# A spectral block on one Trainium2 core: the inverse DFT on 32x64 tiles, the second forward DFT on 64x64 tiles

## The chip, the cores and the metric

The kernel runs on one core of a Trainium2 chip. The metric is device time in microseconds, the median of several executions. Engine names below: TensorE (PE; its weight loads are PEld), VectorE (DVE), ScalarE (ACT), GpSimd (POOL), SyncE (SP, which here only issues DMAs).

## The reference, cut

```python
# x: 4096 rows of 640, all float32
mod = (silu(c) @ w_mod).reshape(1, 6, 1, 640)        # sa, ca, ga, sb, cb, gb
h = layernorm(x) * (1 + ca) + sa
Z = rfft(h, axis=rows).reshape(2049, 4, 160)         # 4 blocks of 160 columns
hr = relu(Z.real @ w1[0] - Z.imag @ w1[1] + b1[0])   # per block, 160 x 160
hi = relu(Z.imag @ w1[0] + Z.real @ w1[1] + b1[1])
or_ = softshrink(hr @ w2[0] - hi @ w2[1] + b2[0], 0.01)
oi_ = softshrink(hi @ w2[0] + hr @ w2[1] + b2[1], 0.01)
x = x + ga * irfft(or_ + 1j * oi_, n=4096)
h = layernorm(x) * (1 + cb) + sb
x = x + gb * ((silu(h @ w_gate) * (h @ w_up)) @ w_down)   # 640 -> 1728 -> 640
```

## The kernel before

The 4096 rows are written as 128 x 32, so that each DFT over rows is done in two factors with a twiddle matrix in the second. The first forward factor (128 points) follows the layer norm and its results go to DRAM (`s1`). Then comes a loop over 8 chunks of frequencies and 4 blocks of columns; a step p is one pair, `ch = p // 4` and `b = p % 4`. The order of instructions on each engine in this part is written out by hand in the loop. The pieces of a step, with the names that the profile shows:

- `load_g` (L310, tile g, SyncE) brings one chunk's rows from `s1`. Partitions hold 32 values of n2 times (parity, real or imaginary part).
- `stage_b(ch, t)` (L636, tile pb), for t = 0 to 4 (four blocks of 128 columns, and the four remainders of 32 columns as t = 4), is the second forward factor: 4 fp32 matmuls of 128 rows, 128 stationary columns and 128 moving columns. An fp32 matmul shows as two records. Its weights are the data; the moving operand is the twiddle table `tb`, which is zero where parities differ. The PSUM bank is b0, or b1 for t = 4.
- `evac_b` (L643 on ScalarE, L644 on VectorE, tile z) scales and splits the result into a high part in fp32r and a remainder. `rem_high`, `rem_low` (L686, L690, tile rt) do it for t = 4, whose rows then go through DRAM to other partitions (`rem_move`, `rem_read`); in the first two chunks `evac_rh`, `evac_rl` (L666, L676, tile rz) do it in place.
- `stage_l1` (L732, tile pl) is the first product: 21 fp32r matmuls into two banks of tag p1 and one of p3. ScalarE takes h (L749, L750) and u (L763) from them, VectorE the low parts (L751) and u (L764); `tail_l1` makes r2.
- `stage_l2` (L800, tile pc, tag p2) is the second product of the step before: 16 fp32r matmuls of 320 columns, two PSUM tiles, each added to the bias into tile tt on VectorE (L802).
- `move_x` (L821, tile xx, SyncE) moves tt by eight DMAs for each chunk, so that real and imaginary parts of 64 frequencies lie on the 128 partitions of one of four tiles xx.
- `shrink_parts` (L827, L828, ScalarE) and `shrink` (L833, or L835 and L836, VectorE) are the soft threshold of one xx; `shrink_high` (L842, ScalarE) and `shrink_low` (L847, VectorE) split it into xh and xl.
- `stage_i` (L858 to L860, tile pi, tag p3) is the first inverse factor of one xx: two halves of 320 columns, each 3 fp32r matmuls with the table `bm` (high and low part). ScalarE evicts to co (L861), and POOL issues the write to DRAM, `s2` (L862).

In a step p of the loop TensorE runs `stage_l1(p)`, `stage_b` of the next chunk (one call, two where b = 1), small sums for the modulation, `stage_l2(p - 1)` and `stage_i(p - 7)`. ScalarE, VectorE and SyncE follow the written order as well; each engine does its queue in order.

The last chunk differs: its inverse runs in fp32 from tt without a move (`inverse_last`, L906, on 64-row halves), in two halves of columns; the first rows of the output are made at once (`first_y`, tile py, L1089 to L1094) with a folded table that takes the last chunk's frequencies straight from tt and the others from `s2` through `load_first_rows` (tile cf, L913, SyncE). `first_stats` and `first_norm` (L1118) normalise them for the FFN, whose first transposes are L1926.

The FFN stage after it is ordered by a planner in the program with costs and due times of its own. It is the larger part of the time.

PSUM has eight banks: two buffers each of p1, p2, p3, and b0 and b1.

Of the kernel before, what the change touches and what calls it, by code (L numbers as in the profile page):

```python
# [6 lines left out]
F32 = mybir.dt.float32  # L7
# [39 lines left out]
def constants():  # L47
# [38 lines left out]
    tb = tb.transpose(0, 3, 1, 2, 4, 5, 6).reshape(8, 4, 128, 128)[ORDER].reshape(32, 128, 128)  # L86
# [3 lines left out]
    tx = tx.transpose(2, 0, 1, 3).reshape(128, 2)  # L90
# [20 lines left out]
    bm = bm.reshape(2, 128, 128)  # L111
    bi = bm[1].reshape(2, 64, 128)

    bx = np.tile(bm[1].reshape(2, 64, 128).transpose(1, 0, 2), (2, 1, 1)).reshape(128, 256)
    bmh, bml = _hl(bm)
    bm = np.stack([bmh, bml], axis=1)
    bm = np.ascontiguousarray(bm.transpose(2, 0, 1, 3)).reshape(128, 2 * 2 * 128)
# [12 lines left out]
    for n in range(4):  # L130
        for h in range(2):
            for r in range(2):
                for i in range(2):
                    m = 4 * (4 * ORDER[-1] + 2 * h + i)
                    ge[64 * i:64 * i + 64, n, 256 * h + 128 * r:256 * h + 128 * r + 128] = (
                        bi[r].reshape(64, 4, 32)[:, :, n] @ ga[n, m:m + 4])
        ge[:, n, 512:] = ga[n]
# [9 lines left out]
        "k_bm": f(bm),  # L147
# [24 lines left out]
def body(tc, x, w1, b1, w2, b2, wg, wu, wd, c, wm, k_fa, k_tb, k_tx, k_bm, k_bx, k_ga, k_ge, k_id, out, dbg=None):  # L172
# [29 lines left out]
    with ExitStack() as top:  # L202
# [3 lines left out]

        def bank0(i, shape, name):
            return ps.tile(shape, F32, tag=f"b{i % 2}", bufs=1, name=name)
# [28 lines left out]
        with ExitStack() as af:  # L237
# [4 lines left out]
            bm = wp.tile([P, 2, 2, 128], F32R, name="bm")  # L242
# [53 lines left out]
            def load_tb(ch):  # L296
                tb = lp.tile([P, 4, 128], F32, tag="tb", bufs=2, name=f"tb{ch}")
                nc.sync.dma_start(tb, k_tb[:, 4 * ch:4 * ch + 4])
                tbs[ch] = tb


            def load_g(ch, lo=0, hi=32, dma=None, cols=(slice(0, D),)):
# [6 lines left out]
                for e in cols:  # L309
                    (dma or nc.sync).dma_start(gs[ch][4 * lo:4 * hi, :, e], src[:, lo:hi, :, e].rearrange("q n j d -> n q j d"))  # L310
# [22 lines left out]
            with tc.tile_pool(name="sp", bufs=1) as sp:  # L333
# [176 lines left out]

            hp = af.enter_context(tc.tile_pool(name="hp", bufs=1, reuse_waits="tile"))
# [20 lines left out]
            bx = p2.tile([P, 2, 128], F32, name="bx")  # L532
# [9 lines left out]
            nc.sync.dma_start(bx.rearrange("p a b -> p (a b)"), k_bx)  # L542
# [17 lines left out]
            def mod_sum(m, hf=0):  # L560
# [3 lines left out]
                elif m in (2, 5):  # L564
                    if m == 5:
                        gbb.append(low_p.tile([P, 320], F32, tag="m", bufs=4, name=f"gbb{hf}"))
                    pm = (bank0(1, [P, 512], f"pm{m}_{hf}") if hf else
                          ps.tile([P, 512], F32, tag="p3", name=f"pm{m}_{hf}"))
                    mm(pm[:, :320], ones, acc[:, 320 * hf:320 * hf + 320], start=True, stop=True)
                    act.activation(gab[:, 320 * hf:320 * hf + 320] if m == 2 else gbb[hf], pm[:, :320], AF.Copy)  # L570
                else:
                    pm = bank0(m, [P, 512], f"pm{m}")
# [55 lines left out]

            def stage_b(ch, t):
                g, tb = gs[ch], tbs[ch]  # L630
                tag = {(0, 1): "p2", (1, 1): "p3"}.get((ch, t))
                pb = (ps.tile([P, 2, 256], F32, tag=tag, name=f"pb{ch}_{t}") if tag else
                      bank0(1 if t == 4 else 0, [P, 2, 256], f"pb{ch}_{t}"))
                col = slice(128 * t, 128 * t + 128)
                for j in range(4):
                    mm(pb[:, :, 64 * j:64 * j + 64], g[:, j, col], tb[:, j, :], start=True, stop=True)  # L636
                pbs[ch, t] = pb

            def evac_b(ch, t):
                pb = pbs[ch, t]  # L640
                z = lp.tile([P, 2, 2, 258], F32R, tag="z", bufs=4, name=f"z{ch}_{t}")
# [4 lines left out]
                if ch == CE:  # L646
                    pool.tensor_copy(z[:, 0, :, 0:257:256], f32(edge[:, 0, t]))
# [10 lines left out]
            def evac_rh(ch, b):  # L658
                pb = pbs[ch, 4]
# [5 lines left out]
                for i in range(2):  # L665
                    act.activation(rzs[ch][32 * i:32 * i + 32, b, 0:256], pb[q, i, :], AF.Identity,  # L666
                                   scale=ca1[q, 4:5])

            def evac_rl(ch, b):
                pb = pbs[ch, 4]  # L670
                r = rzs[ch]
                q = slice(32 * b, 32 * b + 32)
                for i in range(2):
                    rh = slice(32 * i, 32 * i + 32)
                    rl = slice(64 + 32 * i, 96 + 32 * i)
                    dve.scalar_tensor_tensor(r[rl, b, 0:256], pb[q, i, :], ca1[q, 4:5],  # L676
                                             f32(r[rh, b, 0:256]), op0=OP.mult, op1=OP.subtract)
# [6 lines left out]
            def rem_high(ch):  # L684
                rt = rts[ch] = low_p.tile([P, 2, 2, 258], F32R, tag="wt", name=f"rt{ch}")
                act.activation(rt[:, 0, :, 0:256], pbs[ch, 4], AF.Identity, scale=ca1[:, 4:5])  # L686

            def rem_low(ch):
                rt = rts[ch]
                dve.scalar_tensor_tensor(rt[:, 1, :, 0:256], pbs[ch, 4], ca1[:, 4:5], f32(rt[:, 0, :, 0:256]),  # L690
                                         op0=OP.mult, op1=OP.subtract)
# [16 lines left out]
            def stage_l1(ch, b, later=None):  # L708
                NN = width(ch)
                z = zs[ch, b]  # L710
# [4 lines left out]
                for o in range(2):  # L715
# [3 lines left out]
                    seqs.append([(w1a[:, b, cs], z[:, 0, 0, :NN]), (w1a[:, b, cs], z[:, 1, 0, :NN]),  # L719
                                 (w1a[:, b, cl], z[:, 0, 0, :NN]),  # L720
# [241 lines left out]
            for p in range(LAST + 1):  # L962
# [3 lines left out]
                if p < 4:  # L966
                    for f, *a in mods.get(p, ()):
                        f(*a)
# [1596 lines left out]
```

## Time and profile before

| | us |
|---|---|
| median of 3 runs | 1437.01 |
| lowest, highest | 1436.25, 1438.35 |
| span of the profiled execution | 1434.9 |
| spectral stage up to the first forward call of `stage_b` | 0 to 52 |
| loop and tail of the spectral stage | 52 to 311 |
| FFN | 311 to 1435 |

Of the profiled execution only its span is given; launch and end lie around it. In the views, a row has the start or the busy time, the line of the kernel, the operation with the names of its tiles (out<-in), partitions x elements, and a count. In brackets stands how long the engine was idle before it and what ended that. "issue" is time in which the engine waited for nothing that the profile shows. PE records overlap, since their ends are modelled: the distance between starts is what a record costs.

### The profile page before, as it was taken

How to read it: one execution, taken by the hardware profiler on the slowest of the kernel's cores; microseconds unless marked ns; L12 is line 12 of the kernel's file. 1: busy time of each engine (PE TensorE's matmuls, PEld its weight loads, DVE VectorE, ACT ScalarE, POOL GpSimd, SP SyncE). 2: the span in 40 equal slices, each digit the busy share in tenths (PEclk: the TensorE clock that was granted, in tenths of full speed). 3: DMA queues.
4: the chain of work that ended last, by engine and by line, in shares of the span. 5: the costliest groups of instructions: out<-in, count | busy, mean ns of one | idle time of the engine just before them, and what ended most of it. 6: DMA issues, size and time to landing. Idle time of an engine off the chain costs nothing.

```text
span 1434.9 us, 23925 instructions
## 1 busy us (share of the span) xinstructions
PE 1401.5 (98%) x8516; PEld 1327.5 (93%) x8516; DVE 1097.0 (76%) x1978; ACT 783.8 (55%) x1560; POOL 538.0 (37%) x641
## 2 busy tenths in 40 slices
PE   6899999989999999999999999999999999999999
PEld 2699999968989889899999999999999999999998
DVE  8878888778887687767888778888647768567775
ACT  7868878735545555545555556554435345245432
POOL 5300311154444444323244434434324555146533
PEclk9999999999999999999999999999999999999999
DMA  9988798658677989897887997778796666966652
GB/s 377 322 271 259 242 290 275 218 172 263 232 244 277 339 278 298 323 353 243 279 287 253 343 369 251 253 264 290 280 334 233 208 217 240 359 216 222 207 186 89
DMA packets 187383, 382.28 MB, mean 266 GB/s; under 512 B 22240, under 2 KB 104736, under 8 KB 185472
## 3 DMA queue, kind: packets, MB, share of 16 engines
q1 hardware_dynamic: 179072, 364.37, 74.4%
q0 software_dynamic: 6608, 13.77, 3.0%
q10 hardware_dynamic: 1584, 2.62, 0.5%
q8 instruction: 67, 1.10, 0.3%
q14 instruction: 52, 0.43, 0.1%
HBM read 266.66 MB, written 104.86 MB: 259 GB/s over the span
## 4 chain that ended last, share of the span: by engine, by line
PE 78%; DVE 10%; DMA 7%; ACT 2%; issue 1%; SPq 1%; POOL 1%; DVEq 0%; ACTq 0%; POOLq 0%
PE pd L2435 14%; PE pw L2116 8%; PE pw L2118 8%; PE pw L2117 8%; PE pd_X L2297 5%; PE pc L800 4%; PE pl L732 3%; PE pg L1981 3%; PE pg L1980 3%; PE pg L1982 3%; PE pd_Y L2297 3%; PE pw L2127 2%; PE pw L2129 2%; PE pw L2128 2%; DVE st_a L193 2%; DVE wb L1457 2%
## 5 line engine op out<-in xcount | busy, mean ns | idle before, releaser
L2435 PE MATMUL pd<-wdh,a 128*128 128x320 f32 x1040 | 239.2, 310 | 0.6 <-DVE x L2407 0.6
L2435 PEld LDWEIGHTS pd<-wdh,a 128*128 128x128 f32 x1040 | 176.3, 188 | 1.2 <-DVE x L2407 0.9
L2435 PE MATMUL pd<-wdl,a 128*128 128x320 f32 x540 | 166.2, 309 | 0.0
L1457 DVE TENSOR_TENSOR wb<-r,wb 128x512 fp32r<-128x512 f32 (+3 forms) x154 | 155.9, 1023 | 12.0 <-ACT wb L1454 10.3
L2116 PE MATMUL pw<-h,wt 128*128 128x384 f32 x416 | 141.2, 340 | 2.2 <-ACT s_x L2135 2.2
L2118 PE MATMUL pw<-h,wt 128*128 128x384 f32 x416 | 140.2, 337 | 0.0
L2117 PE MATMUL pw<-h,wt 128*128 128x384 f32 x416 | 139.9, 336 | 0.0
L2407 DVE TENSOR_TENSOR x<-x,pd 128x320 f32<-128x320 f32 x240 | 109.2, 478 | 37.8 <-PE pd L2435 33.4
L1454 ACT ACTIVATE wb<-r 128x512 fp32r<-128x512 f32 (+3 forms) x170 | 117.4, 704 | 34.1 <-PE pw L2129 24.3
L2116 PE MATMUL pw<-h,wb 128*128 128x384 f32 x312 | 104.9, 336 | 0.9 <-DVE x L2407 0.9
L2117 PE MATMUL pw<-h,wb 128*128 128x384 f32 x312 | 104.6, 335 | 0.0
L2118 PE MATMUL pw<-h,wb 128*128 128x384 f32 x312 | 104.6, 335 | 0.0
L1980 PE MATMUL pg<-ht,wb 128*128 128x512 f32 x260 | 102.3, 393 | 0.0
L2435 PEld LDWEIGHTS pd<-wdl,a 128*128 128x128 f32 x540 | 101.4, 188 | 0.3
L1982 PE MATMUL pg<-ht,wb 128*128 128x512 f32 x260 | 101.4, 390 | 0.1
L1981 PE MATMUL pg<-ht,wb 128*128 128x512 f32 x260 | 101.5, 390 | 0.0
L2135 ACT ACTIVATE s_x<-pw 128x384 f32<-128x384 f32 x52 | 25.5, 489 | 121.3 <-PE pw L2118 120.2
L1685 POOL TENSOR_TENSOR cr<-cr,gab 128x640 f32<-128x640 f32 x28 | 47.9, 1712 | 99.3 <-DMA cr<-s 86.5
L2116 PEld LDWEIGHTS pw<-h,wt 128*128 128x128 f32 x416 | 78.1, 188 | 3.6 <-ACT s_x L2135 3.6
L862 POOL DMA_DIRECT2D s<-co x28 | 16.0, 571 | 168.1 <-ACT co L861 159.0
L2117 PEld LDWEIGHTS pw<-h,wt 128*128 128x128 f32 x416 | 78.2, 188 | 0.0
L2118 PEld LDWEIGHTS pw<-h,wt 128*128 128x128 f32 x416 | 78.1, 188 | 0.0
(360 smaller groups left out, 4052.7 us busy)
## 6 DMA issues: line engine op xcount, KB each, us to landing
wt<-td SPq DMA_DIRECT2D x104, 512.0 KB, 5.1
hs<-ho SPq DMA_DIRECT2D x52, 512.0 KB, 5.6
h<-hs SPq DMA_DIRECT2D x32, 768.0 KB, 8.8
r<-in_B_w_up_dram SPq DMA_DIRECT2D x36, 640.0 KB, 4.8
r<-in_B_w_gate_dram SPq DMA_DIRECT2D x36, 640.0 KB, 5.3
wdr<-wdd SPq DMA_DIRECT2D x25, 640.0 KB, 5.7
td<-wt SPq DMA_DIRECT2D x25, 512.0 KB, 6.3
g<-s SPq DMA_DIRECT2D x7, 1280.0 KB, 7.4
```

What stands on the lines that cost most here:

```text
L800: mm(pc[:M, :W], l, m, start=(i == 0), stop=(i == len(seq) - 1))
L1454: act.activation(wbs[t, n][:, 0, ks, e], raw[t, n][:, ks, e], AF.Copy)
L1457: (pool if onp else dve).tensor_tensor(wbs[t, n][:, 1, ks, e], raw[t, n][:, ks, e], f32(wbs[t, n][:, 0, ks, e]), op=OP.subtract)
L1980: mm(b, wh, hh, start=(kk == 0), stop=False)
L1981: mm(b, wh, hl, start=False, stop=False)
L1982: mm(b, wl, hh, start=False, stop=(kk == 4))
L2116: mm(b, w(0, kp), a[:, kp, 0], start=start and kp == 0, stop=False, skip_group_check=not start)
L2117: mm(b, w(0, kp), a[:, kp, 1], start=False, stop=False, skip_group_check=not start)
L2118: mm(b, w(1, kp), a[:, kp, 0], start=False, stop=kp == 1, skip_group_check=not start)
L2297: mm(bk[b, i][:, :320], x, y, start=new and j == 0, stop=j == len(seq) - 1, skip_group_check=not new)
L2407: dve.tensor_tensor(x2[:, e], x2[:, e], x[0][:, :320], op=OP.add)
L2435: mm(pd[g, hf][0][:, :320], l, m, start=i == 0, stop=i == len(s) - 1 and not (last and len(gs) > 1))
```

## The change

The second forward factor: `tb` loses its zeros (64 columns instead of 128), the rows of g are laid out with parity first (two DMAs a load instead of one), and each of the 4 matmuls becomes 4 of 64 rows, 64 stationary and 64 moving columns, one for each quarter of the array (parity in rows, half of the 128 columns in columns). Parities write different PSUM banks. Two banks form one tile `bb`, which holds t = 0 and t = 4 together; in the first chunks, banks of p2 and p3 are used for some calls. z is laid out by parity, so that one eviction reads both banks (two where they are not neighbours).

The first inverse factor: no `move_x`, no xx, no split. The threshold works on tt, which is now held in halves of 320 columns (6 buffers). `stage_i(ch, hf)` takes half the columns of a whole chunk: for each of two parts r, two 128-partition tiles q and four groups j of 32 frequencies, an fp32 matmul of 32 rows, 64 stationary and 320 moving columns. The four results lie in two banks of p1 and two of p3. It stands between `stage_b` and `stage_l2`, in every second step, for step p - 5. The last chunk uses the same function; its first half comes ahead of the last `stage_l2`.

```diff
-                pb = (ps.tile([P, 2, 256], F32, tag=tag, name=f"pb{ch}_{t}") if tag else
-                      bank0(1 if t == 4 else 0, [P, 2, 256], f"pb{ch}_{t}"))
-                col = slice(128 * t, 128 * t + 128)
+                if tag:
+                    banks = [ps.tile([P, 2, 128], F32, tag=tag, name=f"pb{ch}_{t}_{p}") for p in range(2)]
+                else:
+                    if t not in (0, 4) or (ch, 4 - t) not in bts:
+                        bts[ch, t] = bp.tile([P, 2, 2, 2, 128], F32, tag="bb", name=f"pb{ch}_{t}")
+                        k = 0
+                    else:
+                        k = 1
+                    bt = bts[ch, 4 - t if k else t]
+                    banks = [bt[:, p, k] for p in range(2)]
+                    pairs[ch, t] = bt[:, :, k].rearrange("c p r k -> c p (r k)")
+                pb = banks
                 for j in range(4):
-                    mm(pb[:, :, 64 * j:64 * j + 64], g[:, j, col], tb[:, j, :], start=True, stop=True)
+                    for d in range(2):
+                        for p in range(2):
+                            h, q = slice(64 * p, 64 * p + 64), slice(64 * d, 64 * d + 64)
+                            mm(banks[p][q, :, 32 * j:32 * j + 32], g[h, j, 128 * t + 64 * d:128 * t + 64 * d + 64], tb[h, j, :],
+                               start=True, stop=True)
...
-                act.activation(z[:, 0, :, 0:256], pb, AF.Identity, scale=ca1[:, t:t + 1])
-                dve.scalar_tensor_tensor(z[:, 1, :, 0:256], pb, ca1[:, t:t + 1],
-                                         f32(z[:, 0, :, 0:256]), op0=OP.mult, op1=OP.subtract)
+                for o, pb in z_pieces(ch, t, 0):
+                    act.activation(o, pb, AF.Identity, scale=ca1[:, t:t + 1])
+                for (o, pb), (h, _) in zip(z_pieces(ch, t, 1), z_pieces(ch, t, 0)):
+                    dve.scalar_tensor_tensor(o, pb, ca1[:, t:t + 1], f32(h), op0=OP.mult, op1=OP.subtract)
...
+            def shrink_parts(ch, i):
+                t = flat(ch, i)
+                act.activation(cl, t, AF.Relu, bias=nlam)
+                act.activation(t, t, AF.Relu, bias=nlam, scale=-1.0)
+
+            def shrink(ch, i):
+                dve.tensor_tensor(flat(ch, i), cl, flat(ch, i), op=OP.subtract)
+
+            def shrink_v(ch, i):
+                dve.tensor_scalar(cl, flat(ch, i), LAM, -LAM, op0=OP.min, op1=OP.max)
+                dve.tensor_tensor(flat(ch, i), flat(ch, i), cl, op=OP.subtract)
+
+            def stage_i(ch, hf, tag=("p1", "p1", "p3", "p3")):
+                e = slice(320 * hf, 320 * hf + 320)
+                if hf == 0:
+                    cos[ch] = [p2.tile([P, D], F32, tag="co", bufs=4, name=f"co{ch}_{j}") for j in range(4)]
+                co = cos[ch]
+                pi = [bank0(0, [P, 512], f"pi{ch}_{hf}_{j}") if tag[j] == "b0" else
+                      ps.tile([P, 512], F32, tag=tag[j], name=f"pi{ch}_{hf}_{j}") for j in range(4)]
                 for r in range(2):
+                    for q in range(2):
+                        for j in range(4):
+                            k = slice(32 * j, 32 * j + 32)
+                            kd = 0 if 4 * ORDER[ch] + j + q == 0 else 1
+                            mm(pi[j][64 * q:64 * q + 64, :320], bx[k, kd, r, :], tts[ch, q, hf][k, r, :],
+                               start=(r == 0), stop=(r == 1))
+                for j in range(4):
+                    act.activation(co[j][:, e], pi[j][:, :320], AF.Copy)
...
+                evac_r(0, 3)
                 tail_l1(0, 0)
                 stage_l1(0, 1)
...
-                on(shrink, p - 6)
+                on(shrink, p - 4)
                 on(stage_l1, p)
...
-                on(shrink_high, p - 6)
...
+                inverse(p - 5)
                 on(stage_l2, p - 1)
-                on(stage_i, p - 7)
-                on(shrink_low, p - 6)
-                if p < LAST:
-                    on(shrink_parts, p - 5)
-                if b == 0 and ch:
-                    for i in range(4):
-                        move_x(ch - 1, i)
+                on(shrink_parts, p - 3)
...
             first_gate_high()
...
+            stage_i(NCH - 1, 0)
+            stage_l2(NCH - 1, 3, [lambda: shrink_v(NCH - 1, 2), lambda: shrink_v(NCH - 1, 3)])
...
-            for i in range(4):
-                if i == 2:
-                    first_norm(2)
-                inverse_last(i, 1)
+            stage_i(NCH - 1, 1, ("p2", "p1", "p1", "b0"))
+            first_norm(2)
```

More of the change, by code (lines that the diff above doesn't have):

```diff
@@ L205, in body @@
         ps = top.enter_context(tc.tile_pool(name="ps", bufs=2, space=PSUM))
+        pools = {}
         def bank0(i, shape, name):
-            return ps.tile(shape, F32, tag=f"b{i % 2}", bufs=1, name=name)
+            return pools["b"].tile(shape, F32, tag=f"b{i % 2}", bufs=1, name=name)
         mhalf = per.tile([P, 8], F32, name="mhalf")
@@ L571, in mod_sum @@
                 else:
-                    pm = bank0(m, [P, 512], f"pm{m}")
+                    pm = ps.tile([P, 512], F32, tag="p1", name=f"pm{m}")
                     for t in range(5):
@@ L658, in evac_rh @@
             def evac_rh(ch, b):
-                pb = pbs[ch, 4]
+                pb = pairs[ch, 4]
                 if b == 0:
```

237 lines of the change are left out of this document (101 added, 136 removed).

## The prediction

> **What bounds the kernel now.** I read the page's span, then the busy time of the stretches, then the chain of waits, then single records where two modes of TensorE meet.
>
> ```profile
> span 1434.9 us, 23925 instructions
> ```
>
> ```profile
> core 0: us, PE busy (x) PEld busy (x) DVE busy (x) ACT busy (x) POOL busy (x), PEclk, DMA share, GB/s
> 72.00:110.00 38.00, 36.93 (x282) 35.81 (x282) 29.79 (x60) 24.77 (x53) 0.00 (x0) 1.00 0.84 265
> 110.00:262.00 152.00, 151.37 (x1178) 150.12 (x1178) 128.97 (x226) 128.33 (x262) 28.24 (x46) 1.00 0.86 268
> 262.00:311.40 49.40, 45.32 (x259) 36.95 (x257) 37.08 (x80) 22.57 (x52) 12.94 (x23) 1.00 0.57 182
> 311.40:1434.90 1123.50, 1111.15 (x6583) 1072.12 (x6582) 839.75 (x1452) 552.83 (x1094) 465.33 (x505) 1.00 0.77 265
> ```
>
> The change lies in 52 to 311 us, the spectral stage (forward calls start at 52); the FFN after it (1123.5 us) isn't edited and is full of TensorE work, so what the stage gains or loses moves the end one for one. From 110 to 262 TensorE is busy 151.4 of 152 us and grants full clock; VectorE and ScalarE have 23 us each to spare. The chain of waits there is TensorE work alone; one block of it:
>
> ```profile
> 242.91 2.52 PE pl L732 x21
> 245.43 0.89 PE pb L636 x8
> 246.32 2.35 PE pc L800 x16
> 248.67 0.14 PE pi L858
> ...
> 249.54 2.52 PE pl L732 x21
> ```
>
> A block costs 6.63 us: first product (pl) 2.52, forward DFT (pb) 0.89, second product (pc) 2.35, six inverse records (pi) 0.87. So in this stretch TensorE time saved or added counts in full. From 262 to 311 TensorE waits:
>
> ```profile
> 263.74 0.41 PE L859 MATMUL pi<-xl,bm 128*128 128x320 f32 x1 [0.46 <-DVE xl L847]
> 284.38 0.42 PE L859 MATMUL pi<-xl,bm 128*128 128x320 f32 x1 [1.06 <-DVE xl L847]
> 288.67 4.04 PE L906 MATMUL pi<-tt,bx 64*128 64x320 f32 x16
> 300.22 1.34 PE L1089 MATMUL py<-cfrm,et 128*128 128x320 f32 x4 [1.81 <-DMA cfrm<-s]
> 305.17 2.32 PE L1092 MATMUL py<-tt,et 128*128 128x320 f32 x8
> 307.96 1.35 PE L906 MATMUL pi<-tt,bx 64*128 64x320 f32 x8
> 311.43 2.56 PE L1926 MATMUL pt<-idn,xn 128*128 128x128 f32 x20
> ```
>
> **What a tile costs.** The last chunk's inverse already runs on 64-row tiles: its eight records at 307.96 take 1.35 us, eight 128-row records of the same 320 columns at 305.17 take 2.32 (0.27 each). Single records at that place:
>
> ```profile
> 307.60 0.43 PE L1094 MATMUL py<-cfrr,et 112*128 112x320 f32 x1
> 307.96 0.53 PE L906 MATMUL pi<-tt,bx 64*128 64x320 f32 x1
> 307.96 0.18 PEld L906 LDWEIGHTS pi<-tt,bx 64*128 64x128 f32 x1 [0.44 <-issue]
> ...
> 307.96 0.55 PE L906 MATMUL pi<-tt,bx 64*128 64x320 f32 x2
> 121.02 1.01 PE pmc L321 x10
> ```
>
> Two things are seen. Records on different row halves start within 0.02 us of each other and then run side by side, so tiles in rows do overlap. And a change of mode drains the array: the last full-size record starts at 307.60 and streams 0.27, yet the first tile load comes at 307.96, so 0.09 is lost, and then the load itself is bare. Ten records with one moving column take 1.01 us: a load of 128 columns is 0.10 and bounds them. A load of 64 columns I take as half, 0.05 (estimate). So entering tiles costs 0.15, leaving them (a 128-column load) 0.20.
>
> **The change part by part.**
>
> Forward DFT (40 calls, 8 chunks by 5). Before: 8 records, 0.89. After: 32 records of 64x64 on four tiles, eight each. Streaming 64 columns is half of the row's 0.11, 0.055. If the four overlap, 8 x 0.055 plus a little skew = 0.50. The floor is 32 starts at 0.013 to 0.02, about 0.43; the ceiling, nothing overlapping, 32 x 0.055 = 1.76; rows overlapping but columns not, 0.9. No row shows two column tiles at once. I take 0.50: each tile has rows, columns and a PSUM half-bank of its own, and the shown overlap of row halves was complete. 40 x (0.50 - 0.89) = -15.6.
>
> Inverse DFT, chunks 0 to 6. Before: 28 x 6 records at 0.146 = 24.6. After: 14 calls of 32 fp32 records on eight 32x64 tiles, four per tile at 0.27 = 1.08, plus skew, 1.2: 16.8. Ends: 1.08, and 2.15 if only row tiles overlap. -7.8.
>
> Last chunk's inverse: 4.04 and about 3.4 (307.96 to 311.43) become two calls of 1.2: -5.0.
>
> Mode changes. Forward calls form 30 groups between full-size work (5 ahead of the loop, 25 in it): 30 x 0.35 = 10.5. In 12 groups an inverse follows in another tile shape: 12 x 0.15 = 1.8. Four inverses in the tail stand alone: 1.4. +13.7. Ends: 0.09 a change if all loads hide (+6), twice my price (+27).
>
> Moves and split. 56 moves (SyncE issues, 160 KB each), the fp32r copy (ScalarE) and the remainder (VectorE) go:
>
> ```profile
> L821 SPq DMA_DIRECT2D xx<-tt x56: 474/594/1654, 93.0 to 268.1; - x56
> L842 ACT ACTIVATE xh<-xx x28: 722/726/742, 104.4 to 285.7; 128x640 fp32r<-128x640 f32 x28
> L847 DVE TENSOR_TENSOR xl<-xx,xh x28: 801/816/2504, 106.0 to 286.4; 128x640 fp32r<-128x640 f32 x28
> L828 ACT ACTIVATE xx<-xx,nlam x23: 830/831/835, 97.8 to 257.4; 128x640 f32<-128x640 f32 x23
> L835 DVE TENSOR_SCALAR cl<-xx x5: 483/486/494, 264.4 to 284.2; 128x640 f32<-128x640 f32 x5
> L836 DVE TENSOR_TENSOR xx<-xx,cl x5: 824/825/826, 264.9 to 284.8; 128x640 f32<-128x640 f32 x5
> ...
> 109.41 0.41 PE L858 MATMUL pi<-xh,bm 128*128 128x320 f32 x1 [0.34 <-DVE u L764]
> 282.90 0.41 PE L858 MATMUL pi<-xh,bm 128*128 128x320 f32 x1
> 310.26 0.92 ACT L1118 ACTIVATE xn<-x,sa,ca 128x640 f32<-128x640 f32 x1 [0.16 <-POOL sa L1112]
> ```
>
> 20 us of ScalarE, 23 of VectorE and 33 of SyncE's queue lie beside TensorE, and no wait from 110 to 262 names the moves' transfers: worth nothing there, neither gain nor loss. What they free is waits: 0.34 at 109, 0.46 at 263.74, 1.06 at 284.38 and, as the last chunk's first half is now inverted before its last second product instead of after, the trip through DRAM, 1.81 at 300.22. A record's tail hides some of each: from 282.90 to 284.38 is 1.48 where 0.15 is usual, 1.33 lost for 1.06 told. With 0.25 added to each: -4.7. Next late there: the soft threshold of the last two tiles, 0.49 + 0.82 each on VectorE after the product's add, ahead of the folded DFT (py): +1.6. And the FFN's first transposes, now 1.5 after the last py instead of 3.4, meet rows that are normalised from 310.26 on, 2.3 after it: +1.5 with the row's own 0.92.
>
> PSUM. This is the added wait. The forward DFT now owns two banks, so the inverse takes two of tag p1 and two of p3, right after the first product has used p1, p1 and one p3:
>
> ```profile
> 209.16 0.29 PE L732 MATMUL pl<-rz,w1c 128*128 128x256 f32 x1
> 210.48 0.38 ACT L763 ACTIVATE u<-pl 64x256 f32<-64x256 f32 x1
> 211.28 0.47 DVE L764 SCALAR_TENSOR_TENSOR u<-pl,b1r,u 64x256 f32<-64x256 f32 x1
> ```
>
> The third bank is free at 211.75 here, 2.5 us after the product, because ScalarE was held by the threshold's two Relus (0.83 in the row above). The fourth inverse tile waits for it, and behind it on TensorE's queue stand the second product and the next block. In the new order the Relus fall at the end of the block before, in blocks without an inverse's evictions; I then get the bank free about 1.2 after the product and the inverse ready 0.8 (single forward call) or 1.3 (double) after it: 12 x 0.35 = +4.2. Ends: 0 and 12 x 1.7 = 20.
>
> Ahead of the loop. The loads of g are two issues instead of one (SyncE, some 0.6 more ahead of the first forward call); two forward calls use two separate banks, so one more ScalarE and VectorE instruction each; and the remainder of block 3 is evicted earlier, ahead of the weight splits that TensorE waits for:
>
> ```profile
> 70.58 0.41 PE L811 MATMUL pc<-w2b,h 128*128 128x320 f32 x1 [1.26 <-DVE w2b L286]
> L676 DVE SCALAR_TENSOR_TENSOR rz<-pb,ca,rz 32x256 fp32r<-32x256 f32 x16 | 7.7, 483 | 2.6 <-ACT rz L666 2.5
> ```
>
> Two of these at 0.48 come in front: +1.0. The four forward calls before 72 us gain nothing, since that wait covers them: +0.9 (four gains of 0.39 given back, less two mode groups). VectorE's and ScalarE's other work keeps its counts, but for two-piece evictions of the remainder (7) and of the chunk with edges: off the path. The write-back of the inverse comes four at a time on POOL, which has 28 of 152 us busy. The moving operand of the first product now lies in two runs of 128; the forward DFT's output before was already in two runs of 64 at 0.11 a record, so I cost that at nothing; the cover, if wrong, is none.
>
> Sum: -15.6 - 7.8 - 5.0 + 13.7 - 4.7 + 1.6 + 1.5 + 4.2 + 1.0 + 0.9 = -10.2. Of the profiled execution the span is given, 1434.9, which becomes 1424.7; the median of the runs, 1437.01, is 2.1 above it (launch and end lie around the span), so 1426.8, said as 1427.
>
> **Weighing two rules.** In "TensorE: Matmul & The Clock Gate" of the Trainium skill, Part 3, a weight load runs beside matmuls in flight only when its row group differs; the two column tiles of one row half would then take turns. The block above speaks against the strict form, since pb's full-height records at 0.11 hide a 0.10 load under the stream of the same rows. The same page's section on the 56 ns gap puts matmul starts never closer than about 25 ns; the pair at 307.96 is closer, on different rows. By it the forward call would be an estimated 0.8 and the sum about +2.
>
> **The rivals.**
>
> Loads take turns (the other side). If the two column tiles of a row half share one path for loads, a forward call is 16 x 0.055 = 0.9, what it was before, and the mode changes are pure loss; the inverse, 0.27 a record, hides its loads. 40 x 0.4 = +16 on the forecast: 1443. It decides from 0.75 a call up, where 40 x 0.25 eats the 10. For it: no row shows column tiles together. Against it: complete overlap of row halves. The first rule above is its strict form.
>
> Issue or PSUM eats it. Either 32 short records can't be fed faster than some 0.025 each (the nearest sustained row is 0.10, so nothing shown excludes it; 40 x 0.3 = +12), or the inverse waits the 1.2 to 1.7 us for the p3 bank as in the row at 211.28 (12 x 1.0 = +12). Each gives 1439: no change. The rule on starts is the first of these.
>
> Columns don't overlap at all: the inverse is 2.15 too, 16 x 0.95 = +15 on top of the 16: 1458.
>
> Nothing waits: PSUM waits vanish and mode changes cost 0.1 (-6): 1417.
>
> **How the numbers follow.** Forecast (1420 to 1433) 0.50; nothing waits 0.15; issue 0.06; PSUM 0.07; loads take turns 0.17; no column overlap 0.05. The measurement tells 0.2%, 2.9 us, from no change. Of issue and PSUM about half is same, a quarter on each side: faster 0.50 + 0.15 + 0.03 = 0.68; same 0.08 (with a corner of the loads that take turns); slower 0.24. The range 1414 to 1442 leaves out the upper part of "loads take turns", the no-overlap case and a tip below. The forecast's own range is 1420 to 1433.
>
> **What would show it.** Right: forward bursts (32 records of 64x64) about 0.5 us long, inverse bursts about 1.2, some 0.15 of idle at each mode change, no moves on SyncE, the first transposes of the FFN near 300 us instead of 311.4, the FFN's length unchanged at 1123. Wrong: forward bursts of 0.8 or more; inverse records with idle before them put down to VectorE's u (the third bank); ScalarE the engine that ends the idle in the loop; a later start of the first forward call by more than a microsecond.

## The result, and the profile after

The change made the kernel slower: 1471.19 us (1469.25 to 1472.87) against 1437.68 (1436.25 to 1440.62) beside it, a ratio of 1.0228 [1.0212, 1.0244]. The forecast was 1427. The profiled execution after has a span of 1468.2 us, 33.3 above the 1434.9 of before.

I cut both spans at the same three places of the program: the first product (pl) of p = 5, that of p = 28, and the FFN's first transposes (pt). The changed kernel's first row starts at 60 us, not at 0. First the kernel before, then the changed one; columns are the stretch, its length, busy time and count of each engine, granted clock, DMA share and GB/s.

```profile
89.50:256.00 166.50, 165.10 (x1281) 163.20 (x1280) 139.67 (x249) 137.60 (x281) 27.69 (x45) 1.00 0.85 262
256.00:311.43 55.43, 51.35 (x307) 42.96 (x305) 42.12 (x88) 28.25 (x64) 13.52 (x24) 1.00 0.59 188
311.43:1434.90 1123.47, 1111.12 (x6583) 1072.12 (x6582) 839.75 (x1452) 552.80 (x1094) 465.30 (x505) 1.00 0.77 265
```

```profile
60.00:117.31 57.31, 32.32 (x370) 29.22 (x371) 30.94 (x58) 26.76 (x59) 10.78 (x7) 0.79 0.62 199
117.31:283.98 166.67, 163.01 (x2235) 144.80 (x2234) 124.63 (x232) 127.85 (x275) 28.42 (x48) 1.00 0.73 208
283.98:334.03 50.05, 45.81 (x385) 36.61 (x383) 32.76 (x72) 20.68 (x47) 10.11 (x18) 0.97 0.52 172
334.03:1468.20 1134.17, 1115.90 (x6590) 1074.53 (x6582) 847.43 (x1458) 553.90 (x1097) 468.04 (x508) 1.00 0.76 262
```

The prediction's own prices can be put on the same cuts (ten forward calls lie in the head, 29 in the loop, one in the tail, which also has the inverse of the last two chunks; of the four waits that were to go, the one at 109.41 lies in the loop):

| stretch | before | after | difference | predicted |
|---|---|---|---|---|
| head, to p = 5 | 89.50 | 117.31 | +27.8 | +0.1 |
| loop, p = 5 to 28 | 166.50 | 166.67 | +0.2 | -1.9 |
| tail, to the transposes | 55.43 | 50.05 | -5.4 | -9.9 |
| FFN | 1123.47 | 1134.17 | +10.7 | +1.5 |

The loop, where nearly all the working went, came out within 2 us of the forecast. The loss lies at the two ends, where TensorE stands. Its waits of more than 2 us between 60 and 117 us in the changed kernel:

```profile
74.80 0.57 PE L839 MATMUL pc<-w2b,h 128*128 128x320 f32 x2 [2.91 <-POOL w2b L279]
...
92.67 1.17 PE L842 MATMUL pc<-w2a,h 128*128 128x320 f32 x3 [12.15 <-DVE tt L854]
...
112.65 1.14 PE L671 MATMUL pb<-tb,g 64*64 64x64 f32 x32 [5.69 <-DVE rz L713]
```

The longest goes back to VectorE. In the kernel before it writes its first two tt without such a wait (first row below); in the changed kernel the second stood 13 us behind a write to DRAM, and that goes back to a row of SyncE's queue:

```profile
71.88 0.93 DVE L812 TENSOR_TENSOR tt<-pc,b2t 128x320 f32<-128x320 f32 x2 [0.57 <-PE pc L811]
```

```profile
78.54 0.49 DVE L854 TENSOR_TENSOR tt<-pc,b2t 128x320 f32<-128x320 f32 x1 [0.79 <-PE pc L853]
92.13 0.49 DVE L854 TENSOR_TENSOR tt<-pc,b2t 128x320 f32<-128x320 f32 x1 [13.09 <-DMA s<-xa]
```

```profile
83.27 0.75 SPq L355 DMA_DIRECT2D s<-xa  x1
```

VectorE's add has nothing to do with `s` or xa: it is waiting for memory. The program's own map of SBUF addresses says which. The tiles xa0 to xa7 hold the input during the first forward factor and are written out to `s1` in an order that follows need; the spectral stage's tiles are later laid over them from the top of SBUF downwards, and each waits for the last reader of what lies beneath:

```
kernel  tile          bytes in each partition  lies over
before  w2a           124864 to 135104         xa1 exactly (w2b xa2, w2c xa3)
before  tt0_0, tt0_1  155584 to 165824         xa4 exactly
after   w2a           134592 to 144832         xa1 and xa2
after   tt0_0_0       165312 to 167872         xa4
after   tt0_1_0       178112 to 180672         xa6, whose last write is issued at 83.27
after   co (four)     183232 to 193472         (later the FFN's hx0_0, 186368 to 188416, and hx0_3, hx0_4)
```

The change dropped xx, xh and xl and added buffers to tt and co. The pool became 7.5 KB smaller, so everything in it moved up by that much against the xa tiles. The FFN's start shows the same thing: ScalarE's hx waits for co to be written out, TensorE for VectorE's ht behind it, and the granted clock halves for ten us (the last two rows below are granted clocks, 0.61 and 0.51, behind the wait of 5.69 and behind this one).

```profile
340.93 0.78 ACT L1930 ACTIVATE hx<-pt,sb,cb 128x512 f32<-128x512 f32 x1 [2.49 <-DMA s<-co]
```

```profile
342.49 0.80 PE L1941 MATMUL pg<-ht,wh 128*128 128x512 f32 x1 [3.26 <-DVE ht L1933]
...
346.99 0.80 PE L1941 MATMUL pg<-ht,wh 128*128 128x512 f32 x1 [1.58 <-DVE ht L1933]
```

```profile
112.60:117.30 4.70, 4.65 (x48) 4.54 (x49) 1.66 (x3) 2.54 (x4) 0.00 (x0) 0.61 0.02 3
342.40:352.00 9.60, 7.93 (x18) 5.81 (x19) 8.80 (x9) 4.57 (x7) 4.02 (x5) 0.51 0.53 161
```

The theory to test was therefore placement, with the one two-bank PSUM tile (the wait of 5.69) as a second cause; the rivals were the loads of g in two transfers, and the tiles themselves.

### The profile page after: what moved, and what is told of

It reads as the page before. It is cut to its first block, busy times and chain, and to the rows that moved or that the text cites. A ratio compares the mean times of both kernels' runs of the same rounds, so it can differ in the third digit from the quotient of the medians.

```text
span 1468.2 us, 26387 instructions
## 1 busy us (share of the span) xinstructions
PE 1404.3 (96%) x9788; PEld 1308.1 (89%) x9788; DVE 1085.3 (74%) x1961; ACT 772.9 (53%) x1552; POOL 538.8 (37%) x640
## 4 chain that ended last, share of the span: by engine, by line
PE 80%; DVE 10%; DMA 4%; ACT 2%; issue 1%; POOL 1%; SPq 0%; ACTq 0%; DVEq 0%; POOLq 0%
PE pd L2434 15%; PE pw L2115 8%; PE pw L2117 8%; PE pw L2116 8%; PE pc L842 5%; PE pd_X L2296 5%; PE pl L774 4%; PE pg L1979 3%; PE pg L1980 3%; PE pg L1981 3%; PE pd_Y L2296 2%; PE pw L2126 2%; PE pw L2128 2%; PE pw L2127 2%; DVE st_a L190 2%; PE py L1701 2%
## 5 line engine op out<-in xcount | busy, mean ns | idle before, releaser
L1456 DVE TENSOR_TENSOR wb<-r,wb 128x512 fp32r<-128x512 f32 (+3 forms) x154 | 152.8, 1003 | 14.9 <-ACT wb L1453 13.5
```

Of the source, the lines that this page charges most:

```text
L1456: (pool if onp else dve).tensor_tensor(wbs[t, n][:, 1, ks, e], raw[t, n][:, ks, e], f32(wbs[t, n][:, 0, ks, e]), op=OP.subtract)
```

## The experiments

Ratios are to the kernel before, run beside each (1438.2 to 1438.9 us).

### Placement: three runs, each the one before plus one shift

An unused tile of 7680 bytes in each partition puts the tiles back. Its position decides which. In all three a second unused tile, between cl and wx, moves acc and cl below the xa tiles. (`...` marks what is left out of the edits shown here and below.)

```diff
 # all three, between cl and wx
+pad = p2.tile([P, 2176], F32, name="pada")
 # e1: behind w2c (w2a, w2b, w2c over xa1, xa2, xa3 again)
+pad = p2.tile([P, 1920], F32, name="padb")
 # e2: instead behind the six tt, which get a tag each so that the first four lie on xa4
-tag="tt", bufs=6
+tag=f"tt{(4 * ch + 2 * (b // 2) + q) % 6}", bufs=1
...
 # e3: instead behind co
```

> The changed kernel with its second weights w2a, w2b, w2c each laid over one x tile again (xa1, xa2, xa3, as in the kernel before), by an unused tile of 7680 bytes a partition behind them; the product's tiles tt and the inverse's outputs co keep their addresses. Placement theory: GpSimd's split of w2a starts at about 60 us instead of 66.18, the 2.91 us that TensorE waits for w2b at 74.80 goes, but the second tt tile still lies on xa6, so TensorE still stands until about 92 and the time falls by 0 to 2 us (1469 to 1471). Rival 'the weights are the whole head': 15 to 25 us less (1446 to 1456). Rival 'traffic' (two issues for each load of g, writes of s1 that land later): nothing moves, 1471.

> As the run before it, and the first four tt tiles now lie on xa4 (written out early) instead of xa4, xa5 and xa6; co keeps its addresses. Placement theory: the wait of 12.15 us ahead of the second product at 92.67 goes, and with it most of the 2.9 ahead of 74.80 and the slow records that follow an idle TensorE (granted clock 0.6 to 0.9): the fifth block's first product starts 14 to 20 us earlier than at 104.37, time 1451 to 1457. Rival 'traffic': the s1 writes land when they land, TensorE waits elsewhere for the loads of g, time 1467 to 1471.

> As the run before it, and the four co tiles lie 7680 bytes lower, so that the FFN's first tiles hx no longer share their memory. Placement theory: ScalarE's first hx no longer waits 2.49 us for the last write of s2, TensorE is not idle 3.3 and 1.6 us at 342 and 347 and keeps full clock: 7 to 11 us less than the run before it (1441 to 1449), FFN from its first transposes 1123 to 1127 us long. Rival 'the FFN starts slowly because its rows x2 come late' (folded rows, statistics): less than 3 us less.

Measured: 1470.01 us, 1.0216 [1.0201, 1.0232]; 1454.46, 1.0108 [1.0088, 1.0127]; 1451.63, 1.0083 [1.0060, 1.0105]. In the first, GpSimd's split of w2a comes earlier (by 3.4 us) and of the wait of 2.91 for w2b 1.60 is left, yet little is gained, and that not clear of the intervals: the wait for tt grows from 12.15 to 14.10.

```profile
62.76 3.62 POOL L279 TENSOR_SCALAR w2a<-rm 128x640 fp32r<-128x640 f32 x2 [21.74 <-DMA rm<-in_A_w_dram]
```

```profile
91.92 1.17 PE L844 MATMUL pc<-w2a,h 128*128 128x320 f32 x3 [14.10 <-DVE tt L856]
```

In the second, VectorE writes both tt at once and the time falls by 15.6 us:

```profile
76.36 0.93 DVE L855 TENSOR_TENSOR tt<-pc,b2t 128x320 f32<-128x320 f32 x2 [0.57 <-PE pc L854]
```

In the third, the FFN starts with a wait of 1.10 where 3.26 stood in the changed kernel and 3.85 in e2. Counted from pt, the 60th of its products starts 6.5 us earlier than in the changed kernel and 3.7 earlier than in e2, and its whole is 1127.82 instead of e2's 1132.24. The medians differ by 2.8 only, and their intervals overlap: 7 to 11 was expected, so this step is shown by the trace and not by the time. (The profiled execution, 1445.7, is the lowest of its four.)

The same cost in the kernel before, whose work is left as it was:

```diff
+p2.tile([P, D], F32, tag="wm", bufs=1, name="wm_")   # takes the memory first, so that tt lies over xa5 and xa6
+for k in range(5):
+    p2.tile([P, D], F32, tag="xx", bufs=5, name=f"xx_{k}")
 first_blocks()
```

> The kernel before, unchanged in its work, with only the addresses of four tags moved: wm and xx take the memory of xa4 and half of xa5, and the two tt tiles lie over xa5 and xa6, where the changed kernel has its first ones. Placement theory: VectorE's second tt waits for the last write of xa6 (issued at 79.45, 7 to 9 us to land) instead of running at 72, TensorE stands 12 to 15 us and its clock falls afterwards: 12 to 18 us slower than before (1449 to 1457). Rival 'it is the change's own work that made the head late' : within 2 us of before.

Measured: 1453.48, 1.0100 [1.0084, 1.0117], 14.7 us for the addresses of three tags (wm, xx, tt) alone. VectorE's first two adds now wait for writes of x rows, and TensorE behind them for 8.28 and 5.54 us:

```profile
79.86 0.49 DVE L812 TENSOR_TENSOR tt<-pc,b2t 128x320 f32<-128x320 f32 x1 [8.70 <-DMA s<-xa]
87.89 0.49 DVE L812 TENSOR_TENSOR tt<-pc,b2t 128x320 f32<-128x320 f32 x1 [7.54 <-DMA s<-rst]
```

For tt, placement is shown from both sides: 15.6 us given back in the changed kernel, 14.7 lost in the kernel before.

### What the tiles cost by themselves

```diff
-for j in range(4):            # stage_b
+for j in [0, 1, 2, 3] * 2:
-for r in range(2):            # stage_i
+for r in [0, 1] * 2:
```

> The third run above with the records of every forward and every inverse call issued twice (the second pass writes the same values again). It prices the tile bursts alone, without mode changes or waits. If all four forward tiles and all eight inverse tiles run side by side, 32 more forward records cost 0.43 to 0.50 us and 32 more inverse records 1.08 to 1.2: 40 x 0.46 + 16 x 1.1 = 36 us more (range 30 to 40). If column tiles of one row half take turns: 0.9 and 2.15, 70 us more.

Measured: 1477.49 (one run), 25.9 above e3's median; its span is 31.8 above e3's profiled one, the lowest of four. 36 was expected (30 to 40), so the total doesn't price the bursts well, since part of the added work can fall where TensorE waits anyway. The trace does. A burst is the distance from its first record to the next product. First e3, then the doubled kernel, the same places:

```profile
214.64 0.69 PE L672 MATMUL pb<-tb,g 64*64 64x64 f32 x32
215.26 0.71 PE L843 MATMUL pc<-w2a,h 128*128 128x320 f32 x3
...
222.71 1.54 PE L885 MATMUL pi<-tt,bx 32*64 32x320 f32 x32
224.18 0.71 PE L843 MATMUL pc<-w2a,h 128*128 128x320 f32 x3
```

```profile
231.49 1.16 PE L672 MATMUL pb<-tb,g 64*64 64x64 f32 x64
232.58 0.71 PE L843 MATMUL pc<-w2a,h 128*128 128x320 f32 x3
...
240.49 2.63 PE L885 MATMUL pi<-tt,bx 32*64 32x320 f32 x64
243.05 0.70 PE L843 MATMUL pc<-w2a,h 128*128 128x320 f32 x3
```

32 more forward records cost 1.09 - 0.62 = 0.47 us (0.50 predicted), 32 more inverse records 2.56 - 1.47 = 1.09 (1.08 to 1.2). Four and eight tiles run side by side. The rivals "loads take turns" and "columns don't overlap" are out, and so is the rival of issue: a record every 0.015 us. "TensorE: Matmul & The Clock Gate" of the Trainium skill has, in Part 1's section on the 56 ns gap, a floor (starts never closer than about 25 ns), by which the forward burst would take an estimated 0.8 us, and in Part 3 the rule that a weight load overlaps only matmuls of another row group, by which both bursts would be longer. The measurement decides here.

### The two-bank PSUM tile

> The changed kernel with one reordering and nothing else: the evictions of chunk 1's remainder for blocks 2 and 3 come inside the head (each pair of ScalarE halves together, then VectorE's), ahead of the fifth block's first product instead of behind it, so that the one two-bank PSUM tile is free when the forward call of chunk 1 for column block 3 is reached. PSUM theory: the 5.69 us ahead of that call (112.65 us) fall to 0 to 1.5, and the clock stays up behind it: 5 to 8 us less, 1463 to 1466. Rival 'VectorE and ScalarE are simply full there': the same wait shows up one call earlier and the time stays at 1470 to 1472.

```diff
-evac_r(1, 0) ... evac_r(1, 1) ... (p == 4:) evac_r(1, 2); evac_r(1, 3)
+evac_rh(1, 0); evac_rh(1, 1); evac_rl(1, 0); stage_l2(0, 2); evac_rl(1, 1); ...   # all ahead of p = 4
```

Measured: 1468.35, 1.0202 [1.0185, 1.0219]: 5 to 8 was expected, 2.8 came, and the intervals of the two kernels overlap. The 5.69 fell to 1.55, but waits of 1.91 and 1.20 rose ahead of it, so the rival has half the truth: eight small evictions that ScalarE and VectorE do in turn (each about 1 us late for the other) are too long for the place, wherever they stand. The next run takes them off PSUM, on top of e3:

```diff
 for t in (4, 0): stage_b(1, t)
+rem_high(1); rem_low(1)                                    # whole tile to SBUF
-act.activation(rzs..., pb[q, ...], scale=ca1); dve.scalar_tensor_tensor(...)
+act.activation(rzs..., rts[1][q, 0, i]); pool.tensor_copy(rzs..., rts[1][q, 1, i])
```

> The kernel with tt and co laid aside (the third run above), and chunk 1's remainder leaves PSUM in two whole-tile passes (ScalarE, VectorE, as later chunks do) into SBUF; the block-by-block pieces are then copied from there, the upper halves by ScalarE, the lower by GpSimd. PSUM theory (the one two-bank tile is held by eight small evictions that ScalarE and VectorE do in turn): the wait of 5.70 us ahead of the forward call at 97.03 falls under 1, the 0.94 ahead of 87.57 and the slow records behind go too: 5 to 8 us less than the third run. Rival 'ScalarE and VectorE are full there': the wait only moves to the next use of a bank, 0 to 2 us less.

Measured: 1449.35, 1.0078 [1.0055, 1.0101], not told apart from e3. The forward call behind no longer waits (5.70 in e3), and the first inverse now waits at a place where e3's trace shows no such wait:

```profile
89.31 1.32 PE L672 MATMUL pb<-tb,g 64*64 64x64 f32 x32 [1.39 <-DVE tt L849]
105.01 1.32 PE L889 MATMUL pi<-tt,bx 32*64 32x320 f32 x26 [2.90 <-DVE u L811]
```

### The inverse's PSUM wait, and order in the head

```diff
 # e6: from p = 4, the first product's narrow group (tag p3) and its eviction ahead of the wide ones
+third(); products(2, 0, 5); third_out()
 # e7: chunk 0's remainder of block 3 behind the second first product
+tail_l1(0, 0); stage_l1(0, 1)
 evac_r(0, 3)
-tail_l1(0, 0); stage_l1(0, 1)
```

> As the run before it, and from the fifth block on the first product's third, narrow group runs ahead of the two wide ones, so that the bank (tag p3) that the inverse waits for is read out about 2 us earlier. Theory of the added PSUM wait: the inverse bursts that follow a single forward call fall from about 1.9 to about 1.45 us and the wait of 1.4 us put down to VectorE's u goes: 2 to 5 us less than the run before it. Rival 'the wide groups' banks are then the late ones' (ScalarE's Relus end at the same time): within 1 us of it.

> As the run before it, and chunk 0's remainder for block 3 is evicted behind the second block's first product instead of ahead of it, so that ScalarE's Relus of that product are not queued behind it. Theory: the 2.16 us that TensorE waits for ScalarE's h at 68.96 falls under 0.7, 1 to 2.5 us less than the run before it, if nothing else is late there; rival 'the next wait takes over' (forward call of column block 3 waits for the same two banks): within 0.7 us.

Measured: 1447.26, 1.0059 [1.0042, 1.0076] and 1446.16, 1.0051 [1.0034, 1.0068]: each 1 to 2 us less than the run before it, which the intervals don't tell apart. The inverse's first wait for u is 2.17 in the trace of the first; the second's shows none there, but e9 below, which has both edits, shows 2.18 again. The second's trace also shows what a short wait costs when the clock goes with it (the usual distance of three products is 0.44; px is the product of ten records with two columns for the edge frequencies, and the last row has the granted clock, 0.50):

```profile
151.04 1.75 PE L921 MATMUL px<-tx,g 128*128 128x2 f32 x10 [1.72 <-DMA g<-s]
152.66 1.15 PE L858 MATMUL pc<-w2a,h 128*128 128x320 f32 x3
153.60 1.00 PE L858 MATMUL pc<-w2b,h 128*128 128x320 f32 x3
152.60:156.00 3.40, 3.40 (x13) 3.40 (x14) 1.25 (x4) 0.00 (x0) 0.58 (x2) 0.50 0.19 74
```

It need not go. In the changed kernel a wait of 1.85 ahead of the same product left the clock at 1.00:

```profile
171.32 1.25 PE L905 MATMUL px<-tx,g 128*128 128x2 f32 x10 [1.85 <-ACT cl L862]
172.43 0.69 PE L842 MATMUL pc<-w2a,h 128*128 128x320 f32 x3
172.40:175.00 2.60, 2.60 (x20) 2.60 (x20) 1.25 (x4) 0.00 (x0) 0.57 (x2) 1.00 0.36 142
```

### The loads of g

```diff
 # b2, in the kernel before: two transfers of half the rows (64 partitions each)
+for l, m in ((lo, mid), (mid, hi)): dma_start(gs[ch][4 * l:4 * m], ...)
 # b3, in the kernel before: two transfers of half the columns (all 128 partitions)
+for h in (left, right): dma_start(gs[ch][:, :, h], ...)
 # e9, on top of e7: load_g and load_tb one block earlier
-if b == 3 and ...
+if b == 2 and ...
```

> The kernel before with each load of g issued as two transfers of half the rows, as many as the changed kernel issues. Theory that the second issue is what makes g late (first forward call 1.75 us later in the changed kernel, chunk 4's load 10.4 to 10.8 us instead of 7.6 from issue to use): 1.5 to 4 us slower (1440 to 1443), a wait for g at the edge product of the thirteenth block. Rival 'the layout of the halves (64 partitions with four rows of two parities), not the number of issues': within 1 us of before.

> The kernel before with each load of g issued as two transfers of half the columns, so that each still fills all 128 partitions. The run with half the rows each was 8 us slower than before, and its halves of 640 KB took 7.7 us to land where the whole load of 1280 KB takes 7.4. Theory that the number of issues is what costs: 5 to 9 us slower again (1444 to 1448). Rival that the half of the partitions is what costs (each transfer then runs on part of the engines that carry it): halves land in 4 to 6 us, 0 to 3 us slower than before.

> The run called e7_rem0_later with each load of a later chunk's g and table issued one block earlier. Theory: the edge product's 1.72 us wait for g at 151.04 and the slow records behind it (products at 1.0 us instead of 0.6) go: 2.5 to 4 us less than that run (1442 to 1444), and the spread of single runs gets narrower. Rival 'the transfer is late because all transfers of that stretch are': the wait moves to another transfer, within 1 us.

Measured: b2 1446.71, 1.0065 [1.0043, 1.0086]; b3 1440.64, 1.0014 [1.0003, 1.0025]; e9 1446.04, 1.0046 [1.0029, 1.0062]. Two transfers of half the partitions cost the kernel before 8 us (1.5 to 4 expected), two of half the columns 2.5. So the number of issues is the smaller part. The rival's price for b3 (0 to 3) held, its landing in 4 to 6 us did not. Size and median time from issue to landing, from the transfers of 100 to 300 us, before, changed, b2 and b3:

```profile
g<-s SPq DMA_DIRECT2D x5, 1280.0 KB, 7.4
```

```profile
g<-s SPq DMA_DIRECT2D x10, 640.0 KB, 8.1
```

```profile
g<-s SPq DMA_DIRECT2D x10, 640.0 KB, 7.7
```

```profile
g<-s SPq DMA_DIRECT2D x10, 640.0 KB, 7.0
```

In each pair the second transfer is issued 0.6 us or more behind the first. By landing alone the halves of b2 and b3 differ by 0.7 us. TensorE's waits put down to g add up to 3.7 us in b2 up to 300 us (before 0.8), so a good part of the 8 us is not traced. In "SBUF — State Buffer" of the Trainium skill, the section on door 1 (the DMA port swizzle) says that partitions 0 to 63 reach 8 of 16 ports, which would make a 64-partition transfer slower in itself; the direction agrees with b2 against b3, and no run here separates the ports from other reasons. Loading earlier (e9) took away the wait for g at the edge product but not the time: the rival held there. The 1.75 us in b2's expectation is not the first forward call, which starts at 51.96 before and at 51.98 after; it is the first product behind it that is 1.6 later (53.87, 55.48).

### Order in the tail, and the last two waits of the head

```diff
 # e10, on top of e9: in the tail the inverse ahead of the sums; in the head evac_b(1, 0) behind stage_l2(0, 2)
-for f, *a in sums.get(p, ()): f(*a)
 if p == LAST + 1: stage_i(NCH - 2, 0)
+for f, *a in sums.get(p, ()): f(*a)
 # f2, on top of e10: bx and wx below the xa tiles, acc over xa0
 # f3: f2 without the edit of e6
 # f5: f2, with chunk 1's upper pieces of blocks 2 and 3 copied by GpSimd instead of ScalarE
```

> As the run before it, with two waits of the trace taken away by order alone: in the last blocks the sums for the FFN's scale come behind the inverse instead of ahead of it (the inverse waits 1.9 us for VectorE's cb), and in the head the high and low split of chunk 1's first column block comes behind the second product (a forward call waits 1.39 us for VectorE's tt at 89.15). Theory: 2 to 3.5 us less than the run before it (1439 to 1441), the kernel before's time. Rival: the next wait takes over, within 1 us.

> The run called e10_tail_order with three tiles exchanged: the inverse's table bx (and wx) lie on memory that no x tile held, the sum acc over xa0 instead. In that run bx was loaded only at 95.85 us, behind the last write of xa0, the scale's weights wm behind it, and the first inverse (4.11 us at 100.12 instead of 1.2) waited for both. Placement theory: bx loads at about 91, the burst falls to 1.2 to 2, 2 to 4 us less than that run: 1437 to 1439, the kernel before's time within 0.2 per cent. Rival 'wm is late because the transfers of that stretch are': within 1 us of that run.

> As the run before it, but with the first product's narrow group last again, as in the changed kernel: prices the PSUM wait of the inverse by itself in a kernel that has no other large wait. Theory of the added PSUM wait: 2 to 5 us slower than the run before it (six to eight bursts of 1.9 instead of 1.45 us, and one longer wait in the head). Rival: within 1 us.

> The run called f2_bx_free with the last four copies of chunk 1's remainder (upper halves, blocks 2 and 3: 1.70 us of ScalarE at 92.29) given to GpSimd, which is idle there. The first inverse waits 1.21 us for ScalarE's h at 97.91 and its burst lasts 2.87 us. Theory that ScalarE is the late engine there: its queue is 1.7 us earlier, the first inverse 1 to 2 us earlier, the time 1 to 2.5 us less than that run (1435.5 to 1437; faster than the kernel before by 0.05 to 0.2 per cent). Rival 'VectorE, which waits 0.88 us for the scale's weights in the same place, is as late': within 0.5 us.

Measured: e10 1440.91, 1.0012 [1.0001, 1.0024], 5 us less than e9 where 2 to 3.5 were expected. f2 1438.00, 0.9994 [0.9982, 1.0007]: 2.9 less than e10, as expected, but the intervals overlap, and the first inverse still lasts 2.8. f3 1442.79, 1.0026 [1.0013, 1.0040]: the inverse's PSUM wait costs 4.8 us here (the same edit gave 2.1 in e6, not clear of noise). Its two rows say it too (idle time ahead of the inverse's matmuls and weight loads together put down to VectorE's u, and how often, 93 to 300 us), f2 then f3:

```profile
  DVE u L794: 2.6, 3
```

```profile
  DVE u L811: 11.8, 11
```

f5 1435.33, 0.9975 [0.9966, 0.9985]: faster than the kernel before by 3 us, a quarter of a per cent, and than the changed one by 36. Its head is 94.43; its other stretches:

```profile
94.43:257.36 162.93, 161.69 (x2236) 144.76 (x2235) 124.09 (x235) 127.92 (x278) 28.80 (x48) 1.00 0.76 219
257.36:304.31 46.95, 44.08 (x384) 35.14 (x383) 32.85 (x72) 20.53 (x47) 10.09 (x18) 1.00 0.53 179
304.31:1434.20 1129.89, 1114.28 (x6590) 1073.47 (x6582) 847.99 (x1458) 554.05 (x1097) 467.97 (x508) 1.00 0.76 263
```

Against before: loop -3.6, tail -8.5, head still +4.9, FFN still +6.4. The change, with these edits, saves 12 us in loop and tail; head and FFN take 11 of it back in this execution.

## Why the prediction was wrong, by its steps

- **"Ahead of the loop", +1.0 and +0.9: the step that failed.** It counted issues and evictions, and the head lost 27.8. Two things were left out. One is where tiles lie: the prediction followed each queue, but not the memory that tiles take over from earlier ones. What removing tiles does to the addresses of the others was put at nothing, without a reason; it moved tt over xa6, and that is 14.7 to 15.6 us by runs in both kernels. It moved w2a over xa2 too, which the trace shows and the time doesn't (1.2 us). The other is bb: t = 0 and t = 4 of a chunk in one tile, evicted by eight small instructions. This is 5.7 of idle time and slow records behind it; the runs could move the wait but show only 2 to 3 us of time for it, not clear of their intervals. The rest of the 27.8 is not priced by a run of its own.
- **Tile bursts: right.** 0.47 and 1.09 for 0.50 and 1.2.
- **Mode changes: too dear.** A forward burst takes 0.62 where its records cost 0.47, and the first product ahead of it lasts 2.58 up to the burst (166.20 to 168.78) where 2.50 stood (138.46 to 140.96): about 0.23 a group for 0.35. That the loop still came out 2 us above its share (+0.2 for -1.9) is because of waits the forecast didn't have, like the 1.85 at 171.32; that it came so close is in part luck.
- **PSUM: right.** The added wait was put at +4.2; f3 against f2 gives 4.8, with some 2.6 of uncertainty on either side. It was in the forecast and so no part of the miss.
- **The loads of g, "some 0.6 more": mis-sized.** A split by partitions cost the kernel before 8 us. How much of the changed kernel's 33 it is can't be read off, since its waits overlap with the others; the changed kernel with one transfer for each load was not run.
- **FFN "length unchanged" but for +1.5: wrong.** The 1.5 came (the transposes meet late rows: in the changed kernel, and in f2, the first FFN product starts 4.46 behind the first transpose, before 2.99), but co under hx and the clock behind it took about 6.5 more in the trace. Some 3 of the 10.7 are left, and the 6.4 of f5 is also more than the 1.5; their cause is open.
- **Tail, -9.9: half.** The waits that were to go there (4.1 of the 4.7) went, but 1.9 for cb (the FFN's scale) and 2.3 in four small ones came. "Next late there" named the threshold, and not the sums for cb, which shared the bank tag p1 with the inverse. With the order changed (and the edits before it) the tail is at -8.5 in f5.
- **The rivals.** All of them were about tiles or PSUM banks in the loop. None was about memory or the ends, so the range (1414 to 1442) had no room for it.
- **The clock** was taken as 1.00 throughout: every wait was priced at about its own length. Behind the longest waits, and behind some of 1.5 to 2 us, it costs more.

Medians add up as follows, from 1471.2 on: weights' placement -1.2, tt -15.6, co -2.8, chunk 1's remainder -2.3, narrow group -2.1, chunk 0's remainder -1.1, earlier g -0.1, order in tail and head -5.1, bx -2.9, copies on GpSimd -2.7. Of the single steps, tt and the order are larger than their intervals, and by f3 the narrow group.

## What to carry to other kernels

When an edit adds or removes on-chip tiles, look up the addresses of all tiles in the pools it touches, before and after, and ask of each early tile who read that memory last and when that transfer lands; a wait of a compute instruction "for a DMA" of a tile it never touches is the sign. Price a wait of TensorE with the slow records that can follow it, and look at the first and last blocks apart from the steady loop. A load cut in two by partitions isn't free, even if the same bytes move (8 us here); cut by columns it costs less (2.5).

## What the runs showed of the hardware

- A record of 64x64x64 on four tiles in turn starts every 0.015 us (0.47 / 32) and one of 32x64x320 on eight every 0.034 (1.09 / 32).
- The granted clock after TensorE stood: 0.61 over 112.6 to 117.3 (after 5.69 us), 0.51 over 342.4 to 352.0 (after 3.26, with a second wait of 1.58 in it), and 0.50 over 152.6 to 156.0 in e7, after a wait of 1.72 and ten records of 2 columns. That wait is shorter than the idle window of about 3.4 us that "TensorE: Matmul & The Clock Gate" of the Trainium skill, Part 1, gives. A wait of 1.85 and the same ten records left the clock at 1.00 in the changed kernel, so the length of a wait alone doesn't decide; what does, no run here shows.
- In the kernel before, a transfer of half the bytes into half the partitions lands no earlier (7.7 us, in b2) than the whole (7.4); half the columns into all partitions lands in 7.0 (b3).
